# The opening of an attention and two-FFN kernel, put in another order

## The chip, the cores and the metric

One core of a Trainium2 chip runs the kernel; every time is device time of that core in microseconds (us). Its engines are TensorE (PE in the rows, PEld for its weight loads), VectorE (DVE), ScalarE (ACT), GpSimd (POOL) and SyncE (SP), which here only issues DMAs. They run side by side, each through its own list of instructions in order, and wait for one another by semaphores. Lower is better; the number compared is the median of several runs.

## The reference

Windowed attention over 4 x 8 heads of 768 tokens with 64 features, then two feed-forward networks without residual:

```
for each chunk c of 32 queries:          # 24 chunks
    keys = 8 memory keys + 16 left + 32 own + 8 right   (64)
    a = softmax(q_c @ keys.T / 8)
    out_c = a @ values
x = out as [3072 tokens, 512]
g = softplus(x @ w1_in);  y = g @ w1_out      # 512 -> 2048 -> 512
h = y @ w2_in;  out = (h - tanh(h)) @ w2_out  # 512 -> 2048 -> 512
```

Weights come as 64-bit floats, the rest as 32-bit.

## The kernel before

**Splitting.** TensorE takes operands rounded to its fast 32-bit format, so each factor of an FFN product is kept as a high part (the rounded value) and a low part (the rest), and a product is three matmuls: high x high, high x low, low x high. A high part is a cast on ScalarE, a low part a subtraction `value - high` on VectorE or GpSimd.

**Units and blocks.** Attention goes in 24 units of 128 tokens; units 0 to 3 make up the first token block of 512. The first FFN has 16 blocks of hidden features, f = 0 to 15; for a token block and each f there is H f (12 matmuls of 512 columns into `ps_h`) and Y f (12 into `ps_y`). The first token block runs in the opening, among the loading and preparing of all of W1 and the attention of units 0 to 7. Everything behind the opening is unchanged by the change.

**The opening is an order written out by hand.** The table OPENING is a string of tokens; the loop below it issues the instructions of each token, and each engine keeps the order in which its own instructions were issued. The tokens, u a unit and f a block:

- qa u, qb u: copy unit u's queries into a padded tile; S u: the score matmuls
- mx u, ex u, ml u: the softmax (function `softmax`). Without `on_act`: VectorE takes the row maximum and subtracts it (L307, L311), ScalarE takes one exponential (L321), VectorE sums (L324) and scales (L325 to L327). With `on_act` the maximum is followed by a small product (L309), ScalarE takes eight exponentials that also sum (L316), and VectorE only scales
- T u: four transposes on TensorE; pT u: ScalarE copies them out (L344); V u: the product with the values; xh u, xl u: its high part (ScalarE, L375) and low part (VectorE, L377)
- y f, s f, h f, l f: weight block f in four steps: scaled copy of the raw bits on ScalarE (L170), the bits put together on VectorE (L185 and two of L189; for f in ASSIST ScalarE does more, L173 and L174, and VectorE one instruction, L178), high part (ScalarE, L196), low part (L198). Block 0 has this apart for its two matrices: yi0, si0, hi0, li0 and yo0, so0, ho0, lo0
- H f, Y f as above; c1 f: softplus of H f (ScalarE, L410), c3 f: its high part gh (L422), c4 f: its low part gl (L427). gh and gl have three buffers each
- Z n: n matmuls of zeros into a bank that nothing reads; L u: loads; K f: stores of prepared weights

H 0 takes all matmuls with the high part of W first, then those with its low part (li0), then those with the low part of x (xl0 to xl3). ON_ACT, ASSIST and ON_POOL are lists of units, blocks and low parts; HOME says into which PSUM bank a token writes. The order of loads (ORDER) is its own list.

**Signals.** An instruction carries a signal only where the builder put one; one that waits for an instruction without a signal of its own waits for the next signal on that engine. In the kernel before, the copy pT0 on ScalarE has none: its count goes up with the last of the eight exponentials of unit 1, which are issued behind it.

Of the kernel before, what the change touches and what calls it, by code (L numbers as in the profile page):

```python
# [45 lines left out]


OPENING = """
Z7 S0 mx0 qa1 qb1 ex0 Z8 S1 ml0 qa2 qb2 T0 mx1 qa3 S2 pT0 qb3 ex1 S3 mx2 mx3 ex2 V0 ml1 ex3 ml2 T1
yi0 ml3 T2 xh0 pT1 xl0 T3 pT2 si0 V1 yo0 pT3 xh1 V3 so0 hi0 y1 li0 V2 xh3 xl1 xh2 xl3 y2 s1 xl2 Z11  # L50
H0 h1 s2 ho0 S4 l1 h2 y3 H1 l2 K1 c10 s3 y4 H2 c30 lo0 h3 c40 c11 l3 Y0 c31 y5 s4 H3 c41 h4 s5 c12
Y1 l4 c13 c32 mx4 c33 h5 c42 H4 y6 l5 y7 s6 H5 c43 h6 s7 Y2 c14 l6 y8 h7 s8 H6 c15 c34 y9 Y3 c44 h8
l7 c16 c35 l8 ex4 H7 s9 H8 c36 c45 y10 c46 ml4 h9 Y4 c17 l9 s10 y12 H9 c18 c37 y11 s12 K2 T4 Y5 pT4
h10 K0 y13 l10 K3 V4 s11 H10 L6 xh4 c47 h11 S5 s13 c19 Y6 K4 mx5 h13 l11 c38 h12 K5 c48 H11 xl4 c110
l12 c39 K6 y14 l13 ex5 H12 s14 K7 Y7 ml5 c49 T5 c310 Y8 y15 c410 pT5 s15 K8 h14 c111 V5 S6 L7 l14
c311 H13 xh5 h15 mx6 c112 l15 c411 K9 H14 c113 xl5 ex6 K10 Y9 ml6 K11 T6 H15 pT6 c312 c412 K12 V6 S7
xh6 L8 Y10 mx7 ex7 c114 ml7 K13 Y11 xl6 K14 T7 c314 Y12 c313 pT7 c413 c115 V7 Y13 xh7 L9 c315 xl7
c414 c415 K15
"""
ORDER = "qk0 qk1 qk2 qk3 v0 v1 i0 v2 v3 o0 w1 w2 w3 qk4 v4 w4 w5 w6 w7 qk5 v5 w8 w9 w10 w11 w12 w13 w14 w15"  # L60
ON_ACT = (1, 3, 4, 5)
ASSIST = (2, 5, 7, 13)
ON_POOL = ('li0', 'l15')
HOME = dict(
    S0="Y0", T0="A0", V0="A", S1="A1", T1="Y10", V1="A",
    S2="Y11", T2="Y01", V2="Y1", S3="Y01", T3="Y00", V3="Y0",
)

TB = 2 * N
# [27 lines left out]
def attention_ffn_ffn(  # L97
# [64 lines left out]
    def low_engine(name):  # L162
        return nc.gpsimd if name in ON_POOL else nc.vector

    def split_w(raw, f, kinds="io", t=None):
# [4 lines left out]
        nc.scalar.mul(w, hi.bitcast(F32), EXP_BIAS)  # L170
        if f in ASSIST:
            x = tpool.tile([P, n, 512, 2], U16, name="c2", bufs=1)
# [88 lines left out]
    def s_mm(u, ps):  # L261
        a = att[u]
        if "apart" in a:
            s = ps.rearrange("p (b a k) -> p b a k", b=2, a=NPAIR)
            for p in range(NPAIR):
                for c in range(NCH):
                    h = 64 * (c % 2)
                    nc.tensor.matmul(  # L268
                        out=s[h : h + 64, c // 2, p],
                        lhsT=a["apart"][:, c, p].rearrange("p j t -> p (j t)"), rhs=a["k"][:, c, p],  # L270
                        start=True, stop=True,
                    )
            a["s"] = s
            return
        for p in range(NPAIR):
            for c in range(NCH):
                for j in range(2):
                    r = slice(64 * j, 64 * j + 64)
                    cc = slice(CHUNK * c, CHUNK * (c + 1))
                    nc.tensor.matmul(  # L280
                        out=ps[cc, j, KEYS * p : KEYS * (p + 1)],
                        lhsT=a["q"][r, p, cc], rhs=a["k"][r, c, p, :],
                        start=True, stop=True,
                    )
        a["s"] = ps[:, :, : NPAIR * KEYS].rearrange("p j (a k) -> p j a k", a=NPAIR)


    def softmax(u, on_act=False):
        a = att[u]
        s4 = a.pop("s")  # L290
        i = u % UPB
        if i == 0:
            nc.vector.memset(s4[0:CHUNK, :, :, NMEM : NMEM + LEFT], NEG)
        if i == UPB - 1:
            nc.vector.memset(s4[P - CHUNK : P, :, :, KEYS - RIGHT : KEYS], NEG)
        if u < UB:
            st, sm = early_st[:, u], early[:, u]
        else:
            st = apool.tile([P, 3, 2, NPAIR], F32, name="st")
            sm = apool.tile([P, 2 * NPAIR * KEYS], F32, name="sm")  # L300
        m, ssum, rec = (st[:, x] for x in range(3))
        a["sm"] = sm
        if "apart" in a:
            smj = sm.rearrange("p (j a k) -> p j a k", j=2, a=NPAIR)
        else:
            smj = sm.rearrange("p (a j k) -> p j a k", a=NPAIR, j=2)
        nc.vector.tensor_reduce(out=m, in_=s4, axis=AX.X, op=ALU.max)  # L307
        if on_act:
            nc.vector.tensor_scalar_mul(m, m, -scale)  # L309
        else:  # L310
            nc.vector.tensor_tensor(out=smj, in0=s4, in1=over_keys(m), op=ALU.subtract)  # L311
        yield
        if on_act:
            for p in range(NPAIR):
                for j in range(2):
                    nc.scalar.activation(  # L316
                        out=smj[:, j, p], in_=s4[:, j, p], func=AF.Exp, scale=scale,
                        bias=m[:, j, p : p + 1], accum_out=ssum[:, j, p : p + 1],
                    )
        else:  # L320
            nc.scalar.activation(out=sm, in_=sm, func=AF.Exp, scale=scale)  # L321
        yield
        if not on_act:
            nc.vector.tensor_reduce(out=ssum, in_=smj, axis=AX.X, op=ALU.add)  # L324
        nc.vector.tensor_scalar_add(rec, ssum, 1e-9)  # L325
        nc.vector.reciprocal(out=rec, in_=rec)
        nc.vector.tensor_tensor(out=smj, in0=smj, in1=over_keys(rec), op=ALU.mult)  # L327
# [499 lines left out]
    with tc.manual_schedule(engines={mybir.EngineType.PE}):  # L827
# [10 lines left out]
        if True:  # L838
# [31 lines left out]
            for token in OPENING.split():  # L870
# [12 lines left out]
                elif op == "S":  # L883
                    s_mm(i, home)
                    going["sm", i] = softmax(i, i in ON_ACT)
                elif op == "T":
# [177 lines left out]
```

## Time and profile before

| | us |
|---|---|
| median of 3 runs | 1057.19 (1055.94 to 1058.36) |
| the profiled execution | 1057.51 |
| its span in the trace | 1055.4 |
| TensorE busy | 1044.2 (99%) |
| VectorE busy | 727.6 (69%) |
| ScalarE busy | 567.1 (54%) |
| GpSimd busy | 7.8 (1%) |

Outside the span lie 2.1 us. TensorE is busy for nearly all of the span, so the end moves by what TensorE waits, by matmuls added, and by its clock. Of the span the opening takes some 120 us; H 0 begins at 28.83 us.

### The profile page before, as it was taken

Reading aid. Unit: us, or ns where it says so; the run is one execution under the profiler, and the core shown is the slowest. Engines: PE = TensorE matmul, PEld = TensorE weight load, DVE = VectorE, ACT = ScalarE, POOL = GpSimd, SP = SyncE. Lnnn points to the kernel's source line nnn. Section 1 sums busy time; section 2 is a strip of 40 time slices with the busy share of each in tenths; the row PEclk is TensorE's granted clock in tenths of the full one; section 3 lists DMA queues with packets and bytes.
Section 4 is the critical chain, followed back from the end, with each engine's and each line's share of the span. In section 5 each row is a group of like instructions: output and inputs, shape, how many; then the busy total and the mean of one; then the engine's idle time right before and its main releaser. Section 6 shows DMA issues by size and latency. Waiting matters only on the chain.

```text
span 1055.4 us, 18458 instructions
## 1 busy us (share of the span) xinstructions
PE 1044.2 (99%) x7368; PEld 857.4 (81%) x7370; DVE 727.6 (69%) x1129; ACT 567.1 (54%) x904; POOL 7.8 (1%) x14
## 2 busy tenths in 40 slices
PE   7999999999999999999999999999999999999998
PEld 5787888888888888888888888888888888888886
DVE  6998445845755657487677687777487877446876
ACT  6996454645656455354454555544455554344553
POOL 2000000000000000000000000000000000000000
PEclk8999999999999999999999999999999999999999
DMA  9989945857777986999987999978799788656651
GB/s 377 407 327 358 337 171 186 301 187 236 263 248 248 312 307 195 341 361 352 325 326 281 359 371 347 341 294 320 272 363 347 293 321 305 224 170 213 243 202 61
DMA packets 101269, 303.19 MB, mean 287 GB/s; under 512 B 8000, under 2 KB 55104, under 8 KB 83520
## 3 DMA queue, kind: packets, MB, share of 16 engines
q1 hardware_dynamic: 101184, 302.02, 79.5%
q8 instruction: 58, 0.95, 0.4%
q14 instruction: 27, 0.22, 0.1%
HBM read 211.29 MB, written 90.70 MB: 286 GB/s over the span
## 4 chain that ended last, share of the span: by engine, by line
PE 97%; DVE 1%; ACT 1%; DMA 0%; issue 0%; ACTq 0%
PE ps_y L387 47%; PE ps_h L387 32%; PE ps_b L387 13%; PE ps_a L361 2%; PE ps_a L280 1%; PE ps_a L332 1%; PE ps_h L880 1%; DMA qk<-in_qk 0%; PE ps_yy L361 0%; PE ps_h L399 0%; DVE gl L427 0%; DVE t L307 0%; DVE x L327 0%; ACT o L170 0%; PE ps_a L268 0%
## 5 line engine op out<-in xcount | busy, mean ns | idle before, releaser
L387 PE MATMUL ps_h<-x,w 128*128 128x512 f32 x900 | 215.3, 390 | 0.1
L704 ACT CAST gh<-w 128x512 fp32r<-128x512 f32 x224 | 139.0, 622 | 140.3 <-DVE gl L645 120.2
L645 DVE TENSOR_TENSOR gl<-w,gh 128x512 fp32r<-128x512 f32 x236 | 163.0, 691 | 71.4 <-ACT gh L704 64.9
L387 PEld LDWEIGHTS ps_h<-x,w 128*128 128x128 f32 x900 | 168.6, 188 | 35.4 <-ACT t L410 0.2
L387 PE MATMUL ps_y<-gh,w 128*128 128x512 f32 x512 | 172.9, 399 | 0.0
L387 PEld LDWEIGHTS ps_y<-gh,w 128*128 128x128 f32 x512 | 96.1, 188 | 21.3
L387 PE MATMUL ps_y<-gh,x 128*128 128x512 f32 x352 | 109.4, 389 | 0.0
L387 PE MATMUL ps_y<-gl,w 128*128 128x512 f32 x256 | 99.7, 390 | 0.0
L387 PE MATMUL ps_y<-w,x 128*128 128x512 f32 x402 | 94.5, 389 | 0.0
L387 PEld LDWEIGHTS ps_y<-w,x 128*128 128x128 f32 x402 | 75.5, 188 | 15.7
L427 DVE TENSOR_TENSOR gl<-t,gh 128x512 fp32r<-128x512 f32 x64 | 45.5, 713 | 55.8 <-ACT gh L422 55.6
L668 ACT ACTIVATE tanh<-sum 128x512 f32<-128x512 f32 x72 | 45.5, 632 | 60.0 <-DVE sum L641 59.8
L387 PEld LDWEIGHTS ps_y<-gh,x 128*128 128x128 f32 x352 | 66.1, 188 | 13.7
L410 ACT ACTIVATE t<-ps_h 128x512 f32<-128x512 f32 x64 | 38.1, 598 | 69.4 <-PE ps_h L387 65.8
L387 PE MATMUL ps_b<-gh,x 128*128 128x512 f32 x176 | 68.5, 389 | 0.0
L387 PE MATMUL ps_h<-gh,x 128*128 128x512 f32 x176 | 68.5, 389 | 0.0
L387 PE MATMUL ps_y<-gl,x 128*128 128x512 f32 x176 | 68.5, 389 | 0.0
L448 ACT CAST o<-c 128x1024 fp32r<-128x1024 f32 (+1 forms) x32 | 31.0, 969 | 69.6 <-DVE c L493 41.1
L645 DVE TENSOR_TENSOR w<-w 128x512 f32<-128x512 f32 x88 | 60.5, 688 | 6.8 <-ACT w L410 5.8
L387 PEld LDWEIGHTS ps_y<-gl,w 128*128 128x128 f32 x256 | 48.2, 188 | 9.0
L387 PE MATMUL ps_y<-x,w 128*128 128x512 f32 x240 | 55.2, 389 | 0.0
L387 PE MATMUL ps_b<-w,x 128*128 128x512 f32 x216 | 54.8, 389 | 0.0
(160 smaller groups left out, 1611.6 us busy)
## 6 DMA issues: line engine op xcount, KB each, us to landing
x<-wod SPq DMA_DIRECT2D x44, 1024.0 KB, 4.7
w<-x2d SPq DMA_DIRECT2D x21, 1024.0 KB, 6.8
x<-wid SPq DMA_DIRECT2D x21, 1024.0 KB, 6.1
wod<-o SPq DMA_DIRECT2D x32, 512.0 KB, 6.1
qk<-in_qk SPq DMA_DIRECT2D x21, 768.0 KB, 6.5
x2d<-o SPq DMA_DIRECT2D x30, 512.0 KB, 7.2
x<-wid SPq DMA_DIRECT2D x18, 768.0 KB, 6.8
ring<-wod SPq DMA_DIRECT2D x12, 1024.0 KB, 5.3
```

Of the source, the lines that this page charges most:

```text
L280: nc.tensor.matmul(out=ps[cc, j, KEYS * p : KEYS * (p + 1)], lhsT=a["q"][r, p, cc], rhs=a["k"][r, c, p, :], start=True, stop=True,)
L332: nc.tensor.transpose(ps[:, p * P : (p + 1) * P], a["sm"][:, p * P : (p + 1) * P], ident)
L361: nc.tensor.matmul(out=ps[h : h + 64, p % 2, 2 * P + t0 : 2 * P + t0 + CHUNK], lhsT=v, rhs=pT, start=True, stop=True,)
L387: nc.tensor.matmul(out=ps, lhsT=a, rhs=b, start=first and i == 0, stop=last and i == 2, skip_group_check=on,)
L410: nc.scalar.activation(out=out, in_=x, func=AF.Softplus)
L427: eng.tensor_tensor(out=gl, in0=t, in1=gh.bitcast(F32), op=ALU.subtract)
L448: nc.scalar.copy(out=hi, in_=src)
L645: nc.vector.tensor_tensor(out=out, in0=x, in1=y, op=ALU.subtract)
L668: nc.scalar.activation(out=t, in_=h, func=AF.Tanh)
L704: nc.scalar.copy(out=gh, in_=src)
L880: nc.tensor.matmul(out=ps_h[1], lhsT=zeros[:, :P], rhs=zeros, start=True, stop=True)
```

## The change

The table OPENING has the same tokens (apart from Z: before 7, 8 and 11 zero products in three places, now 8, 3, 2, 2, 1, 2 and 10 in seven) in another order. ON_POOL gets three more low parts: lo0, l6 and c411 go from VectorE to GpSimd beside li0 and l15. ON_ACT is now units 0, 2, 5 and 6 (before 1, 3, 4 and 5), ASSIST blocks 2, 5, 10 and 11 (before 2, 5, 7 and 13). Some of the first units' PSUM banks differ. Of the table one line of each side stands here; what it does is shown by engine below.

```diff
 OPENING = """
-Z7 S0 mx0 qa1 qb1 ex0 Z8 S1 ml0 qa2 qb2 T0 mx1 qa3 S2 pT0 qb3 ex1 S3 mx2 mx3 ex2 V0 ml1 ex3 ml2 T1
...
+Z8 S0 mx0 qa1 qb1 ex0 Z3 S1 qb2 mx1 qa2 ml0 Z2 S2 qa3 ex1 qb3 T0 mx2 S3 pT0 ml1 ex2 V0 mx3 T1 xh0
...
-ON_ACT = (1, 3, 4, 5)
-ASSIST = (2, 5, 7, 13)
-ON_POOL = ('li0', 'l15')
+ON_ACT = (0, 2, 5, 6)
+ASSIST = (2, 5, 10, 11)
+ON_POOL = ('lo0', 'li0', 'l6', 'c411', 'l15')
 HOME = dict(
-    S0="Y0", T0="A0", V0="A", S1="A1", T1="Y10", V1="A",
-    S2="Y11", T2="Y01", V2="Y1", S3="Y01", T3="Y00", V3="Y0",
+    S0="Y0", T0="A1", V0="Y1", S1="A0", T1="A1", V1="Y0",
+    S2="Y00", T2="A0", V2="Y1", S3="Y01", T3="H0", V3="A",
 )
```

GpSimd, from its last memsets to its end: w0, w6 and w15 are weight blocks 0, 6 and 15, gl a low part of an activation, o_462 and o_424 what block 0's output and input weights are subtracted from.

```order
 L235 MEMSET w12_152 64x16x32 x2
-L198 TENSOR_TENSOR w0_231<-o_417,w0_231 128x512 [waits Activation_49,Pool_49]
-L198 TENSOR_TENSOR w15_1272<-o_1172,w15_1272 128x2x512 [waits DMAHW2_49,DMAHW1_49,DMAHW3_49,PE_49,Activation_49]
+L198 TENSOR_TENSOR w0_231<-o_462,w0_231 128x512 [waits Activation_49,Pool_49]
+L198 TENSOR_TENSOR w0_231<-o_424,w0_231 128x512
+L198 TENSOR_TENSOR w6_779<-o_741,w6_779 128x2x512 [waits DMAHW7_49,DMAHW6_49,Activation_49]
+L427 TENSOR_TENSOR gl_1311<-t_1142,gh_1310 128x512 [waits DVE_49,PE_49,Activation_49]
+L198 TENSOR_TENSOR w15_1316<-o_1012,w15_1316 128x2x512 [waits DMAHW2_49,DMAHW3_49,DMAHW1_49,Activation_49]
```

GpSimd has five subtractions instead of two, and lo0 stands ahead of li0.

VectorE around the softmax of unit 5 (st and sm its sums and values), before: mx5 is L295 to L309, xl4 the L377, s14 the three rows with w14 or o_1108, ml5 L325 to L327.

```order
L295 MEMSET ps_a_86 32x2x4x8 [waits PE_49,Activation_49]
L307 TENSOR_REDUCE st_1072<-ps_a_86 128x8 [waits DVE_49]
L309 TENSOR_SCALAR st_1072<-st_1072 128x8 [waits DVE_49]
L198 TENSOR_TENSOR w11_1020<-o_929,w11_1020 128x2x512 [waits Activation_49]
L427 TENSOR_TENSOR gl_1080<-t_924,gh_1079 128x512 [waits Activation_49]
L377 TENSOR_TENSOR x1_1017<-ps_a_86,x1_1017 128x2x2x128
L198 TENSOR_TENSOR w12_1082<-o_910,w12_1082 128x2x512 [waits Activation_49]
L198 TENSOR_TENSOR w13_1076<-o_958,w13_1076 128x2x512 [waits DMAHW7_49,DMAHW6_49]
L185 TENSOR_SCALAR o_1108<-o_1108 128x1024 [waits Activation_49]
L189 SCALAR_TENSOR_TENSOR o_1108<-w14_225,o_1108 128x1024 [waits DMAHW1_49,DMAHW0_49,DVE_49]
L189 SCALAR_TENSOR_TENSOR o_1108<-w14_225,o_1108 128x1024 [waits DVE_49]
L325 TENSOR_SCALAR st_1072<-st_1072 128x8 [waits Activation_49]
```

The same place now:

```order
L427 TENSOR_TENSOR gl_1087<-t_1071,gh_1086 128x512 [waits Activation_49]
L295 MEMSET ps_a_86 32x2x4x8
L307 TENSOR_REDUCE st_1095<-ps_a_86 128x8 [waits DVE_49]
L309 TENSOR_SCALAR st_1095<-st_1095 128x8 [waits DVE_49]
L377 TENSOR_TENSOR x1_1101<-ps_a_86,x1_1101 128x2x2x128 [waits Activation_49]
L185 TENSOR_SCALAR o_1089<-o_1089 128x1024
L189 SCALAR_TENSOR_TENSOR o_1089<-w14_225,o_1089 128x1024 [waits DMAHW1_49,DMAHW0_49,DVE_49]
L189 SCALAR_TENSOR_TENSOR o_1089<-w14_225,o_1089 128x1024 [waits DVE_49]
L325 TENSOR_SCALAR st_1095<-st_1095 128x8
L326 RECIPROCAL st_1095<-st_1095 128x8 [waits DVE_49]
L327 TENSOR_TENSOR sm_1096<-sm_1096,st_1095 128x2x4x64 [waits DVE_49]
```

xl4 (L377) now stands directly behind mx5 and itself waits for ScalarE; the small product of ml5 (L325) no longer does.

ScalarE at the same place now, where L375 is xh4, L316 the eight exponentials of unit 5 and L410 a softplus:

```order
L422 CAST gh_1086<-t_1071 128x512 [waits PE_49,Activation_49]
L170 ACTIVATE o_1089<-w14_225 128x1024 [waits DMAHW1_49,DMAHW0_49,DVE_49]
L410 ACTIVATE t_1099<-ps_h0_81 128x512 [waits DVE_49]
L375 CAST x1_1101<-ps_a_86 128x2x2x128 [waits DVE_49]
L316 ACT_TABLE_LOAD
L316 ACTIVATE sm_1096,st_1095<-ps_a_86,st_1095 128x64 [waits DVE_49]
L316 ACTIVATE sm_1096,st_1095<-ps_a_86,st_1095 128x64 x7
L410 ACT_TABLE_LOAD [waits PE_49]
```

xh4 stands right ahead of the exponentials. In the built program xh4 carries no signal: ScalarE's count goes from 91 to 100 at the eighth exponential, and xl4 waits for 100.

## Rows read from the trace of the kernel before

**Rows 1.** Busy time of each engine in two stretches; the columns stand in the first line.

```profile
core 0: us, PE busy (x) PEld busy (x) DVE busy (x) ACT busy (x) POOL busy (x), PEclk, DMA share, GB/s
...
30.00:60.00 30.00, 30.00 (x193) 24.54 (x192) 29.61 (x32) 29.54 (x36) 0.00 (x0) 1.00 1.03 409
...
90.00:110.00 20.00, 18.70 (x313) 15.00 (x314) 11.83 (x15) 11.13 (x15) 2.40 (x1) 1.00 0.94 324
```

**Rows 2.** What TensorE waited for, 0 to 200 us: total, times, longest.

```profile
PE ps_yy L332 <- DVE x L327: 1.6, 2, 1.2
PE ps_a L332 <- DVE sm L327: 1.2, 1, 1.2
```

**Rows 3.** Stretches around the clock's fall, columns as in rows 1.

```profile
17.50:20.80 3.30, 1.70 (x38) 1.27 (x37) 3.13 (x9) 2.91 (x12) 0.00 (x0) 1.00 1.02 405
20.80:24.20 3.40, 3.31 (x131) 3.18 (x123) 3.30 (x6) 3.38 (x7) 0.85 (x1) 0.50 1.03 411
24.20:27.60 3.40, 3.07 (x64) 2.17 (x62) 3.04 (x5) 2.30 (x5) 0.81 (x1) 0.50 1.02 408
```

**Rows 4.** Timeline of TensorE: start, length, instruction, idle time before it.

```profile
15.69 1.14 PE L361 MATMUL ps_a<-x,v 64*64 64x32 f32 x64 [0.97 <-ACT x L316]
...
26.10 3.08 PE L880 MATMUL ps_h<-gl 128*128 128x512 bf16 x10 [0.33 <-issue]
28.83 3.10 PE L399 MATMUL ps_h<-x,w 128*128 128x512 f32 x12
31.86 0.86 PE L280 MATMUL ps_a<-qk 64*32 64x64 f32 x64
...
60.02 5.60 PE L387 MATMUL ps_h<-x,w 128*128 128x512 f32 x24
...
105.10 0.63 PE L332 MATMUL ps_a<-ident,sm 128*128 128x128 f32 x4 [1.23 <-DVE sm L327]
```

**Rows 5.** Timeline of ScalarE, pT0 and the end of unit 1's exponentials.

```profile
12.68 0.58 ACT L344 COPY x<-ps_a 128x512 f32<-128x512 f32 x1 [1.16 <-DVE t L307]
...
15.39 0.25 ACT L316 ACTIVATION_READ_ACCUMULATOR x<-ps_a,t 128x1 f32 x1
```

**Rows 6.** Timeline of GpSimd, its two subtractions.

```profile
23.34 1.66 POOL L198 TENSOR_TENSOR w<-o,w 128x512 fp32r<-128x512 f32 x1 [18.71 <-ACT w L196]
97.48 2.40 POOL L198 TENSOR_TENSOR w<-o,w 128x1024 fp32r<-128x1024 f32 x1 [72.48 <-ACT w L196]
```

**Rows 7.** Timeline of VectorE at several places.

```profile
22.45 1.42 DVE L189 SCALAR_TENSOR_TENSOR o<-w,o 128x512 uint32<-128x512 uint32 x2
...
28.48 0.68 DVE L377 TENSOR_TENSOR x<-ps_yy,x 128x512 fp32r<-128x512 f32 x1
...
51.41 1.22 DVE L178 SCALAR_TENSOR_TENSOR o<-o,c 128x1024 uint32<-128x1024 uint32 x1
52.54 1.22 DVE L198 TENSOR_TENSOR w<-o,w 128x1024 fp32r<-128x1024 f32 x1
...
54.40 2.48 DVE L189 SCALAR_TENSOR_TENSOR o<-w,o 128x1024 uint32<-128x1024 uint32 x2
...
57.40 2.35 DVE L198 TENSOR_TENSOR w<-o,w 128x1024 fp32r<-128x1024 f32 x2
...
98.08 2.35 DVE L427 TENSOR_TENSOR gl<-t,gh 128x512 fp32r<-128x512 f32 x1
```

**Rows 8.** Timeline of ScalarE, unit 5's table load and last exponential.

```profile
84.33 1.28 ACT L316 ACT_TABLE_LOAD   x1
...
87.86 0.24 ACT L316 ACTIVATION_READ_ACCUMULATOR sm<-ps_a,st 128x1 f32 x1
```

**Rows 9.** Timeline of VectorE, s14 and the start and end of ml5.

```profile
84.85 0.69 DVE L185 TENSOR_SCALAR o<-o 128x1024 uint32<-128x1024 uint32 x1
85.57 2.48 DVE L189 SCALAR_TENSOR_TENSOR o<-w,o 128x1024 uint32<-128x1024 uint32 x2
88.14 0.17 DVE L325 TENSOR_SCALAR st<-st 128x8 f32<-128x8 f32 x1
...
88.58 0.69 DVE L327 TENSOR_TENSOR sm<-sm,st 128x512 f32<-128x512 f32 x1
```

More of the change, by code (lines that the diff above doesn't have):

```diff
@@ L48 @@
 OPENING = """
-Z7 S0 mx0 qa1 qb1 ex0 Z8 S1 ml0 qa2 qb2 T0 mx1 qa3 S2 pT0 qb3 ex1 S3 mx2 mx3 ex2 V0 ml1 ex3 ml2 T1
[L50 to L58, printed above, removed]
+Z8 S0 mx0 qa1 qb1 ex0 Z3 S1 qb2 mx1 qa2 ml0 Z2 S2 qa3 ex1 qb3 T0 mx2 S3 pT0 ml1 ex2 V0 mx3 T1 xh0
@@ new lines @@
+ml2 ex3 pT1 xl0 Z2 T2 yi0 ml3 V1 yo0 pT2 si0 xh1 Z1 T3 pT3 y1 Z2 V3 so0 hi0 V2 xh3 s1 ho0 xh2 lo0 y2
+li0 K0 xl2 xl3 xl1 Z10 H0 h1 s2 y3 l1 S4 h2 H1 c10 l2 s3 y4 H2 c11 c30 c31 c40 h3 c41 Y0 y5 l3 s4 H3
+c12 s5 h4 Y1 c32 l4 c13 h5 mx4 y6 H4 c42 c33 l5 ex4 s6 H5 y7 c43 h6 Y2 s7 y8 l6 c14 Y3 h7 s8 c15 H6
+y12 c35 l7 c34 h8 c44 H7 c16 l8 y9 c45 y10 s9 H8 ml4 Y4 h9 c17 l9 c36 T4 c46 c37 H9 s10 pT4 c18 K1
+s12 h10 y11 Y5 K2 l10 K3 V4 s11 H10 L6 c47 h11 y15 l11 S5 y13 K4 Y6 h12 c38 l12 K5 c19 H11 c48 c39
@@ L59 @@
+y14 c49 K6 mx5 c110 xh4 H12 ex5 K7 xl4 s14 Y7 c111 ml5 s13 T5 Y8 pT5 c310 K8 c410 h13 V5 c112 l13
+h14 S6 L7 H13 mx6 ex6 l14 s15 K9 H14 xh5 K10 Y9 c311 ml6 h15 c411 xl5 K11 l15 c113 T6 Y10 pT6 K12 S7
+c313 c312 V6 mx7 H15 xh6 L8 c412 ex7 c413 xl6 ml7 Y11 K13 T7 K14 Y12 pT7 c115 c114 V7 Y13 xh7 L9
+c314 xl7 c315 c415 c414 K15
 """
 ORDER = "qk0 qk1 qk2 qk3 v0 v1 i0 v2 v3 o0 w1 w2 w3 qk4 v4 w4 w5 w6 w7 qk5 v5 w8 w9 w10 w11 w12 w13 w14 w15"
-ON_ACT = (1, 3, 4, 5)
-ASSIST = (2, 5, 7, 13)
-ON_POOL = ('li0', 'l15')
+ON_ACT = (0, 2, 5, 6)
```

## The prediction

> **What bounds the kernel now.** I read the busy time by stretch first, then TensorE's waits, then its timeline, and last the lists of the engines that it waits for. From 30 us on TensorE has no idle time but in one place: 30 of 30 us busy from 30 to 60, 18.70 of 20 from 90 to 110 [rows 1]. So the end moves only by when H0 runs and by what TensorE waits behind it. The reader is to see in the same row that from 30 to 60 VectorE is busy 29.61 of 30 us and ScalarE 29.54: they prepare the weights just ahead of TensorE and have no room. What is late for them there becomes a wait of TensorE as soon as their lead is used up. Of waits behind H0 there is one of 1.23 us, before T6, for its softmax [rows 2, 4].
>
> TensorE's clock is the second thing. It is granted in full up to 20.8 us, then at 0.50, the 1.2 GHz level, to 27.6 [rows 3]. Ahead of the fall TensorE was busy 1.70 of 3.30 us, in small pieces, and no single wait was longer than 1.2 us [rows 2, 3]. The ten zero products ahead of H0 took 3.08 us, half of it at the low clock [rows 4].
>
> **The change part by part.**
>
> *Start of H0.* In the new order unit 2 has eight exponentials on ScalarE (2.4 us by those of unit 1: from 13.26, the end of pT0, to 15.64 [rows 5]) ahead of xh0, of unit 3's exponential and of pT1. T2 waits for pT1. Between the end of S2 and T2 so stand 2.4 us, the maximum and subtraction of unit 3 (1.4 us by twice 0.69, as in L327 [rows 9]), an exponential and a copy (0.6 us each): 5.0 us, beside which TensorE has V0, T1 and Z2, 1.14, 0.6 and 0.9 us. TensorE then waits some 2.4 us, twice the longest wait of before. Behind it ml3 (0.69 + 0.17 + 0.20 + 0.69 = 1.75 us, its first by L327's duration, the others by rows of the kind [rows 9]) comes after xl0 on VectorE instead of ahead, and si0, so0, s1 and the last three low parts follow as before. The last low part of x ended at 28.48 + 0.68 = 29.2 [rows 7]; it ends near 31.0 now. The last four matmuls of H0 need it, so H0 ends near 32.1 instead of 31.86 [rows 4], where S4 began: +0.2 us.
>
> To this comes GpSimd. Its li0 stands behind lo0, at about 1.2 us each by half of the 2.40 us for 1024 columns [rows 6], and lo0's high part comes while VectorE runs the two L189 of s1, 1.24 us each [rows 7]. GpSimd's first subtraction of before took 1.66 us for 512 columns: it began at 23.34 in the middle of an L189 that ended at 23.87, and 23.87 + 1.2 is its end [rows 6, 7]. The other one ran from 97.48 to 99.88, and VectorE's L427, 0.69 us elsewhere, took 2.35 us, from 98.08 to 100.43 [rows 6, 7]: it waited until GpSimd was through. So the two engines exclude each other in instructions that read two tiles of SBUF, whichever began first going on. For the start this means one L189 behind lo0 and li0 behind that L189: 1.2 us more on VectorE's chain at most, 0 if they miss each other. I take 1.0: VectorE has L189s for 2.5 us there. The term is **+1.2** (0.2 to 1.4), and VectorE begins the next block, l1, 1.5 us later than before.
>
> *l6 on GpSimd.* In the old order l7 ended at 57.40 + 1.2 = 58.6 and H7, which begins at 60.02, needs it for its third matmul at 60.5 [rows 4, 7]: a lead of 1.9 us. Now: VectorE begins 1.5 us later, TensorE 1.2 later; lo0 and l6 leave VectorE (0.6 and 1.1 us of its time); block 7 leaves ASSIST, so s7 takes 0.69 + 2.48 us instead of 1.22 [rows 7, 9], 1.9 more; unit 4's softmax leaves ScalarE, which adds a subtraction, 0.5 net. That leaves 1.9 - 1.5 + 1.2 + 1.7 - 1.9 - 0.5 = 0.9 us. But l6 holds GpSimd for 2.4 us while VectorE runs s7, L189s, each of which reads two tiles. The row of before lost 1.66 us having come 0.6 after GpSimd's start [rows 6, 7]; one that comes at once loses 2.3. Lead 0.9 - 2.1 = -1.2: TensorE waits **1.2 us** in H7 (0, if L189 isn't held up, to 1.6).
>
> The Trainium skill (SBUF — State Buffer, § Who interferes with whom) says that a VectorE instruction with two SBUF inputs and a GpSimd instruction that reads SBUF exclude each other, and that one-input shifts and copies in the two-port modes do too. The held L427 agrees, 1.66 us; that an L189 or L185 is held no row shows. By the rule the two terms stand as taken; if only the kind in the row were held, they would be 0.2 and 0, and the sum 2.2 us less.
>
> *Unit 5 on ScalarE, and s14.* On VectorE, xl4 now follows mx5, then s14, then ml5. xl4 needs xh4 alone, but xh4 has no signal, and xl4 waits for the count that the last of unit 5's exponentials sets. That such a wait is real, the trace shows: V0 needs pT0, which ended at 13.26, and began at 15.69, with the last exponential's end at 15.64 [rows 4, 5]. Before, s14 (0.69 + 2.48) ran beside the exponentials, and ml5 began at 88.14, right at their end [rows 8, 9]. Now it can't. I count from the end of Y6, which gives back the buffer for the gh of c39: c39 0.6, c49 0.7, mx5 1.0, table load 1.28, exponentials 2.5 (85.63 to 88.10 [rows 8]), xl4 0.68, s14 3.17, ml5 1.1 (88.14 to 89.27 [rows 9]), eight handovers of about 0.1: 11.8 us less 0.4 for what overlaps, 11.4. TensorE has H11, H12 and Y7 to do meanwhile, 2.73 each by 24 matmuls in 5.46 to 5.60 us [rows 4]: 8.2. T5 waits **3.2 us** (0, if the wait ends at xh4, to 3.6). It cannot be hidden: Y8 and H13 stand behind T5 in TensorE's list.
>
> *What goes.* T6's 1.23 us go, since unit 6 has no subtraction and its chain begins earlier: **-1.2**. Unit 7's becomes the late one: from V6's end maximum, subtraction, table load, exponential, sum, two small ones and the product are 6.1 us with handovers, H15 and Y11 5.5: **+0.6** (0 to 1.2). c411 and l15 run beside PSUM-reading work of VectorE or none: 0 (up to 0.7).
>
> *Zero products and the clock.* Two more are 0.9 us, inside waits: 0. The stretch with the 2.4 us wait is emptier than the one that made the clock fall before, so it falls again; T3, V3, V2 and Z10 then run at 1.2 GHz, Z10 4.3 us instead of 2.2, and H0 begins near 30.8 instead of 28. As li0 and the last low part of x set H0's end anyway, I take **+0.5** (0 to 1.5). The Trainium skill (TensorE: Matmul & The Clock Gate, § The HAM clock gate) lets the clock fall after an idle window; here it fell although TensorE was busy half of the time ahead of it and waited 1.2 us at most [rows 2, 3]. By the rule it would stay up here, and the sum would be 0.5 lower.
>
> Sum: 1.2 + 1.2 + 3.2 - 1.2 + 0.6 + 0.5 = +5.5 us. The profiled execution took 1057.51 us (span 1055.4 and 2.1 outside it), so this one would take 1063.0; it stands 0.3 above the median of the runs, so for the median I say **1062.7 us**.
>
> **Rivals.** (a) *Engines don't block each other in s1 and s7*: the two terms fall to 0.2 and 0, and 1060.5 remains. For it: held L189s are not in the trace. Against: GpSimd waited for one. (b) *The clock stays low longer*, because zeros in twos and threes don't bring it back before H0: H0 itself then takes up to 2.7 us more, of which the late li0 covers half: 1064.5. For it: at the low clock small products filled 3.31 of 3.40 us and it stayed low [rows 3]. (c) *VectorE's relief counts* and the kernel gets faster: 0.6, 1.1 and 0.6 us leave the engine that is 99% busy, the zeros hold the clock at 2.4 GHz, and H0 begins at 27 instead of 28.83 with its inputs there; from there the place that decides is T5: if xl4 runs right behind xh4, s14 is over when the exponentials end, T5 finds its softmax ready, and T6's 1.2 is gain: -1.8 - 1.2 = 1054.2. Against it: the built program's count. (d) *It comes to nothing*: TensorE's waits of 1.2 and 3.2 overlap, since every wait gives VectorE and ScalarE time to get ahead, and half of the sum is left behind the start's gain: within 2 us, 1057.5.
>
> **How the numbers follow.** The forecast 0.46, (a) 0.18, (b) 0.17, (c) 0.08, (d) 0.11. About 0.2% or 2.1 us is what a measurement of this kernel tells from no change, 1055.1 to 1059.3. Slower is the forecast, (a) and (b): 0.81; the same is (d), 0.11; faster is (c), 0.08. The range of 1057 to 1066.5 leaves out (c) and a tenth more above and below; its upper end is the sum of the upper bounds of the start, H7 and the clock (+1.6) on (b).
>
> **What would show it.** TensorE's waits after: one of some 3 us before T5 for VectorE's L327, near 92 to 96 us; one of about 1 us inside H7, near 62, for an L198; none before T6. VectorE: an L189 of 2 us or more beside a GpSimd L198 near 54; xl4 (L377) waiting some 4 us for L316. A wait of over 2 us before T2 near 17 to 20 us, and S4's start at 33 or later instead of 31.86. If S4 begins before 31.5 and T5 doesn't wait, the forecast is wrong as a whole; if T5 waits and H7 doesn't, it is (a).

## The result and the profile after

The changed kernel takes 1065.07 us (median of 6 runs, 1064.38 to 1066.08), the kernel before in runs beside it 1057.32: a ratio of 1.0072, interval 1.0061 to 1.0083. The forecast was 1062.7, in the range 1057 to 1066.5: slower, as said, by 7.75 us instead of 5.5. The profiled execution took 1064.66 us with a span of 1062.7.

In the two profiled executions nearly all of it arises before 134 us. S8, the first scores of the main loop, begins at 133.13 us and began at 125.89, 7.24 later; what follows takes 929.57 us after and took 929.51. So S8's start serves below as the meter of a profile. In the kernel before it is this row of TensorE's timeline (columns as in [rows 4]):

```profile
125.89 0.86 PE L280 MATMUL ps_a<-qk 64*32 64x64 f32 x64
```

TensorE's timeline after, T2 first, then Z10, the two parts of H0, S4, H7, T5, T6, T7 and S8. The brackets hold its waits and what ended them; the list of its waits from 19 to 200 us has no others.

```profile
19.49 1.11 PE L332 MATMUL ps_a<-ident,x 128*128 128x128 f32 x4 [3.07 <-ACT x L344]
...
27.11 2.33 PE L880 MATMUL ps_h<-gl 128*128 128x512 bf16 x10
29.09 1.27 PE L399 MATMUL ps_h<-x,w 128*128 128x512 f32 x4
31.25 2.09 PE L399 MATMUL ps_h<-x,w 128*128 128x512 f32 x8 [0.89 <-POOL w L198]
33.27 0.86 PE L280 MATMUL ps_a<-qk 64*32 64x64 f32 x64
...
63.07 5.29 PE L387 MATMUL ps_h<-x,w 128*128 128x512 f32 x22 [1.02 <-DVE w L198]
...
96.59 0.63 PE L332 MATMUL ps_a<-ident,sm 128*128 128x128 f32 x4 [3.63 <-DVE sm L327]
...
111.64 0.60 PE L332 MATMUL ps_a<-ident,sm 128*128 128x128 f32 x4
...
123.08 0.63 PE L332 MATMUL ps_a<-ident,sm 128*128 128x128 f32 x4 [0.53 <-DVE sm L327]
...
133.13 0.86 PE L280 MATMUL ps_a<-qk 64*32 64x64 f32 x64
```

Against [rows 4]: S4 is 1.41 us later, H7 waits 1.02 and T5 3.63, T6's 1.23 are gone and T7 waits 0.53. VectorE (s1's pair of L189, the last low part of x, s7's pair, then T5's chain) and GpSimd at these places:

```profile
26.31 2.49 DVE L189 SCALAR_TENSOR_TENSOR o<-w,o 128x1024 uint32<-128x1024 uint32 x2
...
29.91 0.68 DVE L377 TENSOR_TENSOR x<-ps_yy,x 128x512 fp32r<-128x512 f32 x1
...
54.04 4.72 DVE L189 SCALAR_TENSOR_TENSOR o<-w,o 128x1024 uint32<-128x1024 uint32 x2
...
91.58 0.69 DVE L377 TENSOR_TENSOR x<-ps_a,x 128x512 fp32r<-128x512 f32 x1 [4.23 <-ACT sm L316]
...
92.91 2.48 DVE L189 SCALAR_TENSOR_TENSOR o<-w,o 128x1024 uint32<-128x1024 uint32 x2
...
95.75 0.69 DVE L327 TENSOR_TENSOR sm<-sm,st 128x512 f32<-128x512 f32 x1
```

```profile
27.58 3.61 POOL L198 TENSOR_TENSOR w<-o,w 128x512 fp32r<-128x512 f32 x2 [22.95 <-ACT w L196]
54.01 2.40 POOL L198 TENSOR_TENSOR w<-o,w 128x1024 fp32r<-128x1024 f32 x1 [22.82 <-ACT w L196]
```

At 27.58 GpSimd waited until VectorE's pair ended at 28.80 and then ran lo0 and li0, 1.2 us each, to 31.19; at 54.01 it was first, and VectorE's pair took 4.72 instead of 2.48: held by 2.24. At 91.58 xl4 follows the last exponential, then come s14's pair and ml5, and T5 follows L327.

The busy times around T5 (columns as in [rows 1]; the first number behind POOL's pair is the granted clock):

```profile
92.90:96.60 3.70, 0.07 (x2) 0.04 (x1) 3.58 (x6) 0.56 (x1) 0.00 (x0) 1.00 1.03 372
96.60:99.00 2.40, 2.40 (x10) 1.97 (x11) 2.33 (x3) 1.10 (x2) 0.00 (x0) 0.67 0.08 33
99.00:101.40 2.40, 2.40 (x8) 1.69 (x6) 1.89 (x3) 1.80 (x3) 0.00 (x0) 0.62 0.00 0
```

This the forecast did not have: TensorE, idle from 92.96 to 96.59 in T5's wait, is granted 0.67 and 0.62 behind it, that is, mostly the 1.2 GHz level. From T5 to T6, 15.05 us here, experiment 1 takes 13.46 without the fall: 1.59. Together: 1.41 + 1.02 + 3.63 + 1.59 - 1.23 + 0.53 = 6.95 of the 7.24 us; T2's wait and the low clock of the start are in the 1.41, and 0.29 is not assigned.

### The profile page after: what moved, and what is told of

It is laid out like the page before. It is cut to its first block, busy times and chain, and to the rows that moved or that the text cites. A ratio compares the mean times of both kernels' runs of the same rounds, so it can differ in the third digit from the quotient of the medians.

```text
span 1062.7 us, 18462 instructions
## 1 busy us (share of the span) xinstructions
PE 1045.2 (98%) x7372; PEld 857.6 (81%) x7372; DVE 725.6 (68%) x1126; ACT 570.4 (54%) x906; POOL 13.7 (1%) x17
## 4 chain that ended last, share of the span: by engine, by line
PE 92%; DMA 4%; DVE 3%; ACT 1%; issue 0%; SPq 0%; DVEq 0%; ACTq 0%
PE ps_y L387 46%; PE ps_h L387 29%; PE ps_b L387 13%; DMA w<-in_w1i 2%; PE ps_a L361 2%; PE ps_a L280 1%; DVE o L189 1%; DMA qk<-in_qk 1%; PE ps_a L332 1%; DMA w<-in_qk 1%; DVE w L198 0%; DVE o L185 0%; ACT sm L316 0%; DVE st L307 0%; DVE gl L427 0%
## 5 line engine op out<-in xcount | busy, mean ns | idle before, releaser
L427 DVE TENSOR_TENSOR gl<-t,gh 128x512 fp32r<-128x512 f32 x63 | 43.1, 688 | 52.1 <-ACT gh L422 51.9
L410 ACT ACTIVATE t<-ps_h 128x512 f32<-128x512 f32 x64 | 38.1, 597 | 65.6 <-PE ps_h L387 65.0
```

The source lines that it names most:

```text
L410: nc.scalar.activation(out=out, in_=x, func=AF.Softplus)
L427: eng.tensor_tensor(out=gl, in0=t, in1=gh.bitcast(F32), op=ALU.subtract)
```

## The experiments

Each ratio is to the kernel before, on the same chip; "after" is the changed kernel (1.0072).

**1. T5's wait.** In the order of after:

```
-xh4 H12 ex5 K7 xl4 s14
+xh4 xl4 H12 ex5 K7 s14
```

> Unit 4's low part xl4 stands ahead of unit 5's exponentials in the order instead of behind them; all else as in the changed kernel (1065.1 us). Theory: T5's wait of 3.63 us exists because xl4 waits for the count that the last exponential of unit 5 sets, with s14 and ml5 queued behind it; and TensorE's clock falls behind T5 only because of that wait, which costs some 1.7 us more in Y8 (12 products in 4.4 us instead of 2.7). Then xl4 runs near 88 us without a wait, s14 beside the exponentials, T5 waits under 0.5 us, the granted clock stays at 1.00 from 90 to 110, and the time is 1065.1 - 3.6 - 1.7 = 1059.8 us. Rival A, unit 5's eight exponentials on ScalarE are themselves the late thing: T5 still waits over 2 us and the time is 1063 to 1065. Rival B, the clock falls there for another reason: the wait goes and the clock still falls, 1061.5. Rival C, what is gained is lost at T6 and T7, whose softmaxes have no more lead: waits of 1 to 2 us there and 1061.5 to 1062.5.

Measured: 1059.09 us, ratio 1.0021 (1.0012 to 1.0030): 6.0 less. VectorE, then TensorE's S4, T5, T6 and S8, then a stretch around T5:

```profile
87.05 0.69 DVE L377 TENSOR_TENSOR x<-ps_a,x 128x512 fp32r<-128x512 f32 x1 [0.45 <-ACT x L375]
```

```profile
32.65 0.86 PE L280 MATMUL ps_a<-qk 64*32 64x64 f32 x64
...
92.13 0.63 PE L332 MATMUL ps_a<-ident,sm 128*128 128x128 f32 x4
...
105.59 0.60 PE L332 MATMUL ps_a<-ident,sm 128*128 128x128 f32 x4
...
127.06 0.86 PE L280 MATMUL ps_a<-qk 64*32 64x64 f32 x64
```

```profile
90.00:100.00 10.00, 10.00 (x166) 8.04 (x165) 9.20 (x14) 7.58 (x14) 0.00 (x0) 1.00 0.84 303
```

xl4 waits for its own copy, T5 for nothing, and the clock stays at 1.00. S8 comes 6.07 us earlier than in after: 3.63 for the wait, 1.59 for the clock, and 0.62 because S4 came earlier in this execution; 0.23 is left over. Rivals A, B and C fall: the eight exponentials themselves are early enough.

**2. The clock without the wait's end.** The order has `N15` ahead of T5, 15 products of x's tile into the bank that T5 overwrites.

```
+elif op == "N":
+    for _ in range(i):
+        nc.tensor.matmul(out=ps_a[:, 0], lhsT=x_tile(0)[:, 0, 0, :P],
+                         rhs=x_tile(0)[:, 0, 0, :], start=True, stop=True)
```

> The changed kernel with 15 products of x's own tile, thrown away, in TensorE's list right ahead of T5 (about 15 x 0.23 = 3.4 us, by the 512-column products of Y7), so that TensorE is busy in the wait of 3.63 us; the wait itself stays. Theory: T5 begins at the same 96.6 us, the granted clock stays at 1.00 behind it instead of 0.67 and 0.62, and Y8 takes 2.7 us instead of 4.4: 1065.1 - 1.7 = 1063.4 us. Rival: Y8 is slow for its operands or for VectorE's and ScalarE's work beside it, or the clock falls anyway: 1065.1. Second rival: the products delay the release of a buffer and T5 begins later, 1066 or more.

Measured: 1063.38, ratio 1.0064 (1.0051 to 1.0076), 1.7 less; the interval overlaps that of after, so the rows have to decide.

```profile
34.50 0.86 PE L280 MATMUL ps_a<-qk 64*32 64x64 f32 x64
...
93.89 3.56 PE L885 MATMUL ps_a<-x 128*128 128x512 f32 x15
97.59 0.66 PE L332 MATMUL ps_a<-ident,sm 128*128 128x128 f32 x4
...
111.11 0.60 PE L332 MATMUL ps_a<-ident,sm 128*128 128x128 f32 x4
```

```profile
90.00:100.00 10.00, 9.86 (x46) 7.89 (x45) 7.12 (x10) 5.62 (x21) 0.00 (x0) 1.00 0.80 306
100.00:110.00 10.00, 10.00 (x165) 8.18 (x164) 9.20 (x14) 8.20 (x24) 0.90 (x1) 1.00 0.69 243
```

T5's softmax is as late as before, the clock stays at 1.00, and from T5 to T6 it is 13.52 us, as in experiment 1. T5 came 1.00 later than in after because S4 was 1.23 later in this execution (why, see 4). So the wait costs 3.6 as a wait and 1.6 as the cause of a clock fall.

**3. l6.** `ON_POOL` without `'l6'`.

> The changed kernel with l6 back on VectorE (four low parts on GpSimd). Theory: GpSimd's l6 (2.40 us) holds one L189 of s7 by 2.24 us, more than the 1.13 us that l6 costs VectorE itself; without it no L189 of s7 takes over 1.3 us, l7 ends 1.1 us earlier and H7's wait of 1.02 us goes or falls under 0.2: 1064.1 us (1064.0 to 1064.4). Rival: H7 waits because VectorE comes late out of the start and s7 lost ScalarE's help, and l6 on GpSimd is a relief: the wait grows by 1.1 to some 2.1 us and the time to 1066.2.

Measured: 1063.73, ratio 1.0063 (1.0050 to 1.0077), 1.3 less; this interval too overlaps that of after. In the rows H7 has no wait, the pair that took 4.72 takes 2.48, and T4, with S4 at 33.26 as in after (33.27), begins at 69.98 instead of 70.92:

```profile
54.20 2.48 DVE L189 SCALAR_TENSOR_TENSOR o<-w,o 128x1024 uint32<-128x1024 uint32 x2
```

```profile
69.98 0.60 PE L332 MATMUL ps_a<-ident,sm 128*128 128x128 f32 x4
```

The low part on GpSimd held VectorE by more (2.24) than such a subtraction takes on VectorE (1.22 [rows 7]). In this profiled execution the gain is lost again behind T5, where the clock fell for longer: 16.02 us from T5 to T6.

**4. The start: GpSimd's order, no GpSimd, a filled pause.** Experiment 4 moves lo0 and K0 behind H0:

```
-V2 xh3 s1 ho0 xh2 lo0 y2 li0 K0 xl2 xl3 xl1 Z10 H0 h1 s2 y3 l1
+V2 xh3 s1 ho0 xh2 y2 li0 xl2 xl3 xl1 Z10 H0 h1 s2 y3 lo0 K0 l1
```

> The changed kernel with lo0, and the store K0 that needs it, moved behind H0, so that GpSimd's li0 stands alone ahead of H0 (in the changed kernel the two together run from 27.58 to 31.19 and H0's last eight products begin at 31.25). Theory 1, GpSimd can't begin until VectorE's pair of L189 of s1 is over at 28.8: li0 ends near 30.0, the last low part of x at 30.6 as now sets H0's end, S4 begins at 31.7 to 32.0 instead of 33.27, and the time is 1065.1 - 1.4 = 1063.7 us. Theory 2, whichever engine begins first goes on: li0 begins near 26.2 behind its high part, ahead of the first L189, holds it by 1.1 us, the last low part of x ends near 31.7, S4 begins near 32.7: 1064.5 us. Rival: H0's end is set by something else (the clock, a transfer): S4 stays at 33.2 and the time at 1065.1.

Experiment 5 has `Z13` instead of `Z2` ahead of T2:

> The changed kernel with 13 zero products instead of two ahead of T2, so that TensorE is busy through its wait of 3.07 us for pT1 (11 more, 0.22 us each, 2.4 us). Theory: the clock fell at 18.9 because of that wait; now the granted clock stays at 1.00 from 16 to 30, V1, T3, V3 and V2 end some 1.5 us earlier, and VectorE's low parts of x, which wait for ScalarE's copies of them, gain about half of it until GpSimd's two subtractions set H0's end: S4 at 32.2 to 32.7 instead of 33.27, 1065.1 - 0.8 = 1064.3 us (1064.0 to 1064.8). Rival A: VectorE's own 20 instructions set H0's end whatever the clock does: S4 at 33.2, 1065.1. Rival B: the clock falls in spite of the products: granted clock 0.50 from 20 to 25 again, no change.

Experiment 6 has `ON_POOL = ('l6', 'c411', 'l15')` and the order `li0 xl2 xl3 xl1 lo0 K0`:

> The changed kernel with li0 and lo0 on VectorE, li0 ahead of the last three low parts of x and lo0 behind them (with the store K0); l6, c411 and l15 stay on GpSimd. Theory, as the prediction put it, the start's lateness is GpSimd's and VectorE's excluding each other: without them li0 is over at 29.5, the last low part of x ends near 31.2 and S4 begins at 32.3 to 32.6 instead of 33.27: 1065.1 - 0.8 = 1064.3 us. Rival: what counts from H1 on is VectorE's sum of work; the two subtractions cost it 1.3 us, l1 comes later by as much, S4 begins earlier but a new wait of 0.7 to 0.9 us stands in H1 for l1 (L198 on VectorE): 1065.0 to 1065.3.

Measured: 4: 1065.4 us, 1.0080 (1.0068 to 1.0093). 5: 1065.85, 1.0077 (1.0058 to 1.0097). 6: 1064.7, 1.0070 (1.0051 to 1.0089). None can be told from after by its time; the profiles tell more, but S4 differs between executions of one start as well. GpSimd, VectorE and S4 in experiment 4:

```profile
26.20 1.28 POOL L198 TENSOR_TENSOR w<-o,w 128x512 fp32r<-128x512 f32 x1 [21.56 <-ACT w L196]
27.66 2.04 POOL L198 TENSOR_TENSOR w<-o,w 128x512 fp32r<-128x512 f32 x1 [0.19 <-ACT w L196]
...
26.30 4.49 DVE L189 SCALAR_TENSOR_TENSOR o<-w,o 128x1024 uint32<-128x1024 uint32 x2
...
33.78 0.86 PE L280 MATMUL ps_a<-qk 64*32 64x64 f32 x64
```

li0 began 0.1 us ahead of the pair, which took 2.0 longer; lo0, still next in GpSimd's own list, came in between the two L189s. S4 is later than in after: theory 2, with both low parts instead of one.

Experiments 1 and 2 run the instructions of after up to S4. GpSimd and s1's pair in 1, then Z10 and a stretch of H0 in 2:

```profile
26.42 4.14 POOL L198 TENSOR_TENSOR w<-o,w 128x512 fp32r<-128x512 f32 x2 [21.78 <-ACT w L196]
...
25.96 3.45 DVE L189 SCALAR_TENSOR_TENSOR o<-w,o 128x1024 uint32<-128x1024 uint32 x2
```

```profile
27.32 4.45 PE L880 MATMUL ps_h<-gl 128*128 128x512 bf16 x10
...
28.00:30.00 2.00, 2.00 (x6) 0.76 (x5) 2.00 (x3) 2.00 (x3) 2.00 (x2) 0.50 1.01 401
```

In 1 the pair took 0.97 more than alone and li0 ended at 30.56, 1.15 behind it: one L189 behind lo0, and li0 behind that L189, as the prediction had it. GpSimd came 1.16 earlier there than in after, in the middle of the pair's first L189; the granted clock from 20 to 26 us, by twos, was 0.72, 0.50 and 0.93 there against 0.50, 0.50 and 0.57, and ScalarE's copies ahead of lo0's high part wait for TensorE. In 2 the clock was still at 0.50 when H0 began, and S4 came at 34.50. So the same start put S4 at 32.65, 33.27 and 34.50, the later the longer the clock was low.

In experiment 5 the clock stays up and H0 begins 2 us earlier, to wait for li0:

```profile
22.00:24.00 2.00, 1.76 (x66) 1.25 (x65) 1.90 (x5) 1.50 (x2) 0.00 (x0) 1.00 1.02 406
```

```profile
27.12 1.28 PE L399 MATMUL ps_h<-x,w 128*128 128x512 f32 x4
30.63 2.09 PE L399 MATMUL ps_h<-x,w 128*128 128x512 f32 x8 [2.23 <-POOL w L198]
32.65 0.86 PE L280 MATMUL ps_a<-qk 64*32 64x64 f32 x64
```

S4 is 0.62 earlier than in after, but not than in experiment 1. T5 to T6 took 16.16 us here (15.05 in after, 16.02 in experiment 3): the loss behind T5 is 1.6 to 2.7 us by execution, a spread larger than the 0.8 that the time should show. S4 and the rest of H1 in experiment 6:

```profile
32.05 0.86 PE L280 MATMUL ps_a<-qk 64*32 64x64 f32 x64
33.78 5.29 PE L387 MATMUL ps_h<-x,w 128*128 128x512 f32 x22 [0.21 <-DVE w L198]
```

S4 is 1.22 us earlier than in after, of which H1 gives back 0.21 (the rival had 0.7 to 0.9). Half of it goes with the clock: in experiment 1, whose Z10 began at 25.95 and took 2.33 as here at 26.09, S4 came at 32.65. GpSimd's two subtractions so cost 0.60.

**5. Adding the mends.** Experiment 7 joins experiment 1, 3 and 5 and writes `T6 S7 Y10 pT6 mx7` for `T6 Y10 pT6 K12 S7 ... mx7`. (S7 then overwrites unit 6's transposed probabilities before they are copied: that part of the order serves for its time alone, the instructions are the same.)

> The changed kernel with four edits: xl4 ahead of unit 5's exponentials, l6 back on VectorE, 13 zero products ahead of T2, and S7 with unit 7's maximum ahead of Y10 so that T7's wait of 0.53 us goes. If the terms add up: 1065.1 - 6.0 (xl4, measured) - 1.3 (l6, measured) - 0.5 (T7) - 0.8 (start) = 1056.5 us, 0.7 below the kernel before (1057.25); TensorE has no wait over 0.3 us between 34 and 240. Rival: the gains overlap, since each wait that goes leaves VectorE and ScalarE less lead for the next: a wait of 1 us or more shows at H7, T6 or T7 and the time is 1057.5 to 1058.5.

Measured: 1059.39, ratio 1.0014 (1.0001 to 1.0027). No wait at H7, T5, T6, T7, a clock of 1.00 in the profiled execution, and still S4 at 32.68. The sum was 2.9 us too low. The profiled execution (1057.57) is one of four with a mean clock of 0.999 to 1.000 (1057.01 to 1058.56); the other eight, at 0.997 or 0.998, took 1059.11 to 1060.62. So the clock goes with most of what they lost; no profile shows where it fell.

Experiment 11 is experiment 5 with `ON_ACT = (0, 5, 6)`, experiment 12 joins 1, 3, 6 and 11:

> The changed kernel with the filled pause ahead of T2 (13 zero products) and unit 2's softmax back on VectorE (one exponential of 512 columns on ScalarE and a subtraction of 0.69 us on VectorE instead of eight exponentials of 64). With the pause alone filled S4 began at 32.65 us at a clock of 1.00. Theory, as the prediction put it: unit 2's eight exponentials, 2.4 us of ScalarE ahead of xh0, unit 3's exponential and pT1, delay T2; without them T2 begins at 18.8 or earlier instead of 19.54 and S4 near 31.9: 0.7 us less than with the filled pause alone, 1064.3 us. Rival: VectorE's subtraction costs as much as ScalarE gains, T2 stays at 19.5, S4 at 32.6, 1065.

> The changed kernel with the mends together: xl4 ahead of unit 5's exponentials, li0, lo0 and l6 on VectorE (lo0 behind the low parts of x), unit 2's softmax on VectorE, 13 zero products ahead of T2. Theory: the terms add up, 1065.1 - 6.0 - 1.3 - 0.8 - 0.7 - 0.5 = 1055.8 us (1055.5 to 1056.6), S4 near 31.2, no wait over 0.6 us from H1 to T6 and 0.5 before T7: with T6's 1.2 us gone it stands level with the kernel before at full clock (1056.1). Rival: four more low parts on VectorE, which is 94% busy from 30 to 60 in the changed kernel, come back as waits in H1 to H7: 1057.5 to 1059.

Measured: 11: 1066.02, 1.0075 (1.0063 to 1.0088). 12: 1057.6, 0.9996 (0.9987 to 1.0005). In 11 T2 stayed at 19.48, now behind its own zero products, and

```profile
29.87 3.66 PE L399 MATMUL ps_h<-x,w 128*128 128x512 f32 x8 [2.02 <-POOL w L198]
```

```profile
30.00:32.00 2.00, 2.00 (x5) 1.56 (x6) 2.00 (x3) 1.66 (x3) 0.00 (x0) 0.51 1.04 416
```

H0's rest begins 0.76 earlier than in 5, as expected, but the clock is low behind H0's own pause of 2.02 us: 3.66 us instead of 2.09. The time does not decide it; unit 2's share stays open. Experiment 12 brings the new order level with the kernel before, not below it; and its 11 executions, all at a clock of 0.999 or 1.000, took 1056.53 to 1059.07, where the kernel before took 1056.05 to 1056.45 in its four of that clock beside it.

**6. The kernel before.** Experiment 8: `ON_POOL = ('li0',)`, and `H14 ex6 c113 xl5` for `H14 c113 xl5 ex6`. Experiment 9: zero products `Z3` ahead of V0, `Z5` of T2, `Z1` of T3, `Z2` of V3. Experiment 10: both.

> The kernel before with l15 on VectorE instead of GpSimd and unit 6's exponential one place earlier (ahead of c113). Theory: T6's wait of 1.23 us in the kernel before comes from l15 on GpSimd, which held VectorE's L427 by 1.66 us, and from the exponential behind a softplus and its table load; without both the wait goes: 1057.25 - 1.2 = 1056.0 us (1055.9 to 1056.6). Rival: l15's 1.2 us on VectorE and the later c113 make another thing late (Y9, H15): 1057.0 to 1057.8.

> The kernel before with 11 more zero products in the pauses of its opening (three ahead of V0, five ahead of T2, one ahead of T3, two ahead of V3), nothing else: the one part of the change that fills pauses, alone. In the executions of the kernel before so far the mean granted clock was 0.994 to 0.997 with 1057.1 us and more, or 0.999 to 1.000 with 1055.9 to 1056.4: in some the clock falls in the opening, in others not. Theory: the pauses decide it; with them filled the clock stays at 1.00 in every execution, S4 begins at 29.6 to 29.9 (as in the run of the kernel before without l15 on GpSimd, whose clock stayed up) instead of 31.86, and the median is 1056.1 us (1055.9 to 1056.6) instead of 1057.4. Rival A: the clock falls in the same share of executions, or the products delay V0 and T2: 1057.3 to 1058. Rival B: the clock doesn't count, since VectorE sets H0's end: 1057.3 with a clock of 1.00.

> Both that gained in the kernel before: the filled pauses of its opening, and l15 on VectorE with unit 6's exponential ahead of c113. Theory: the two add, clock 1.00 and no wait before T6 in every execution: 1057.3 - 1.3 - 1.3 = 1054.7 us (1054.4 to 1055.2), below both kernels. Rival: in half of the executions the clock falls all the same: 1055.6 to 1056.2.

Measured: 8: 1056.11, 0.9983 (0.9971 to 0.9996). 9: 1057.47, 0.9996 (0.9987 to 1.0005). 10: 1055.63, 0.9980 (0.9971 to 0.9988), below both kernels, though 0.9 above its sum. S4 and T6 in 8, then S4, T6 and a later product in 9:

```profile
29.58 0.86 PE L280 MATMUL ps_a<-qk 64*32 64x64 f32 x64
...
102.03 0.60 PE L332 MATMUL ps_a<-ident,sm 128*128 128x128 f32 x4
```

```profile
30.13 0.86 PE L280 MATMUL ps_a<-qk 64*32 64x64 f32 x64
...
103.84 0.63 PE L332 MATMUL ps_a<-ident,sm 128*128 128x128 f32 x4 [1.29 <-DVE sm L327]
...
139.85 0.50 PE L387 MATMUL ps_y<-gh,w 128*128 128x512 f32 x1 [0.72 <-DVE o L441]
```

In 8 T6 has no wait. Its two edits lie on one chain of the kernel before: c113, the softplus ahead of unit 6's exponential on ScalarE, had waited 2.64 us for the L427 that l15 held:

```profile
100.54 0.60 ACT L410 ACTIVATE t<-ps_h 128x512 f32<-128x512 f32 x1 [2.64 <-DVE gl L427]
```

Experiment 8 takes both away; which of the two would do alone was not run. In 9 the theory held for the clock, 0.999 to 1.000 in all 11 executions, and fell for the time: they took 1057.05 to 1058.39, the kernel before's four of that clock 1056.05 to 1056.45. The products make S4 0.55 later than in 8, and behind S8 (124.63) come 930.8 us instead of 929.5, with a wait for L441. What L441 itself waited for, in the list by line (idle us, times):

```profile
DMA y1d<-o: 3.6, 1
```

Its buffer was still being stored. An early end of the opening is not the reason: in 8 and 10 S8 comes earlier still, at 122.78 and 123.11, 929.6 us follow, and there is no such wait, while experiment 12, with S8 at 126.14, has one of 0.7. The reason stays open.

## Why the prediction was right, and where its sizes were off

- *Start of H0, +1.2:* 1.41, the start's clock included. T2's wait of 2.4 us was 3.07, the last low part of x ended at 30.59 (forecast 31.0). The exclusion came as forecast in experiment 1, which runs the same start; in the profiled execution of after GpSimd came later, held no instruction of VectorE's pair and waited itself. In both it was not the last low part of x that H0 waited for but li0, ahead of its last eight products, not four. The two subtractions on GpSimd cost 0.60 (experiments 6 and 1). The base hides some of the new start's cost: with the clock up in both, S4 comes at 32.65 (experiment 5) and in the old order at 29.58 (experiment 8), 3.07 apart.
- *l6, +1.2:* 1.02, by the mechanism given, L189 held by 2.24 (forecast 2.1); without it H7 has no wait. Rival (a), engines that don't block each other, falls.
- *T5, +3.2:* 3.63, xl4 waiting 4.23 for the last exponential. Taking it away took the wait away.
- *What goes, -1.2 and T7, +0.6:* -1.23 and +0.53. c411 and l15 on GpSimd cost no wait, as said.
- *Zeros and the clock, +0.5:* about right in size for the start: the clock fell as forecast (0.50 from 20 to 24 us), and one that stays up is worth 0.62 in S4 against after (experiment 5), 0 against experiment 1 and 1.85 against experiment 2. What the sum left out is a second fall: it priced T5's wait at its length alone, and the clock's fall behind it at nothing. That fall cost 1.59 us in the profiled execution and 1.6 to 2.7 in others, most of the difference between +5.5 and 7.24.
- *Rival (b)*, a clock that stays low into H0, named the time within 0.6 us (1064.5), but in the profiled execution H0 ran at full clock; in experiment 2's it did not. By its own terms (half of 2.7 us on 1062.7) it comes to 1064.1, and the upper end of the range, 1.6 above the 1064.5 given, to 1066.1, not 1066.5. The range was made wide for a low clock in the start and in H0, not for one behind T5; that it held the result is in so far luck.
- *Rivals (c) and (d)* fall with T5's wait. What spoke for (c) is true of the kernel before in another way: its T6 wait went by giving l15 back to VectorE and moving one exponential (experiment 8).

The Trainium skill (SBUF — State Buffer, § Who interferes with whom) says that of VectorE and GpSimd the one that issues first goes on and the other blocks fully. The rows agree: GpSimd, 0.03 us ahead at 54.01, held the pair by 2.24, and at 27.58, with the pair running since 26.31, it waited 1.2 itself.

## What to carry to other kernels

Ask of each wait what it does to the clock behind it as well as how long it is. An instruction that waits for a count waits for all that was issued before that count on the other engine: look what is queued in between, and move the waiter ahead of it. An engine that excludes a busy one in some instructions, as GpSimd does VectorE here, relieves it only where its instructions miss the other's. Where one kernel runs at more than one clock, compare executions of the same clock.

## What was not expected of the hardware

The clock in the opening differs between executions of one kernel. Of 23 executions of the kernel before beside experiments 5 to 8, ten had a mean granted clock of 0.999 to 1.000 and took 1055.90 to 1056.37 us, the others 0.994 to 0.997 and 1057.31 to 1061.66. The rows of its profile in front of the prediction are one of the second kind; experiment 8, whose opening is the same up to S4, shows the first (S4 at 29.58 instead of 31.86). The Trainium skill (TensorE: Matmul & The Clock Gate, § The HAM clock gate) calls the gate's warm-up at a kernel's start variable from run to run; what varies here is a fall in mid-opening, which that sentence does not cover. Experiment 9, with the pauses filled, had all of its 11 executions at 0.999 or 1.000, where the kernel before beside it had 4 of 27: with these pauses filled the clock did not fall. Why it falls in some executions with the pauses and not in others stays open.
